# Nine operations moved in a written-out order, and five of 35 warm-up products left out, in a one-core attention and feed-forward kernel

## The chip, the core and the metric

The kernel runs on one core of a Trainium2 chip. The core has a matrix engine (TensorE, PE in the profile; its weight loads are listed apart as PEld), a vector engine (VectorE, DVE), a scalar engine (ScalarE, ACT), GpSimd (POOL) and SyncE (SP), which in this kernel issues nearly all transfers. Each engine works through its own queue in order; engines wait for each other through semaphores. The metric is the device time of one execution in microseconds. The kernel before took 210.79 us (median of three runs, 210.59 to 211.69).

## The reference

Attention over 4 sequences of 768 positions with 8 heads of 64, in which a position sees the 8 first positions and the 95 before it, with a linear bias by distance; then a feed-forward layer, softplus between two products, over the 3072 tokens.

```python
scores = scale * np.matmul(q, k.transpose(0, 1, 3, 2)) + bias      # bias = -slope(head) * distance
scores = np.where(is_global | is_local, scores, -1e9)
a = softmax(scores)                                                # max-subtracted, +1e-9 in the sum
x = np.matmul(a, v)  ->  (3072, 512)                               # heads side by side
h = x @ w_in                                                       # 512 -> 2048
g = np.maximum(h, 0.0) + np.log1p(np.exp(-np.abs(h)))              # softplus
out = g @ w_out                                                    # 2048 -> 512, float32
```

## The kernel before

**Blocks, units, groups.** The tokens are cut into 24 blocks of 128, numbered n = 0 to 23 in the order of work. Two neighbouring blocks of a sequence are a unit (12 units, i); the q, k and v of a unit are loaded together. Block n lies in unit n // 2. Two blocks are also a group (12 groups, g) of the feed-forward layer, whose 256 tokens go through it together. So unit 7 is the blocks 14 and 15, and unit 6 is the blocks 12 and 13, which begin a sequence.

**Names of the operations.** Every piece of work has a name, and the table `ORDER` gives each name an engine (P, V, A, G, S for PE, DVE, ACT, POOL, SP). For a unit i: `ldq`, `ldk`, `ldv` are its loads (L609, 512 KB each, from SP); `castq`, `castk` make bf16 copies (L675, L687); `castv7.11` and its like make the bf16 copy of v in four pieces, the first digit after the dot being the block of the unit and the second one of two halves of its rows (L707); `trq`, `trk7.0`, `trk7.1` are transposing transfers that put q and k into the layout for the products (L837, L830). For a block n: `sc` is its scores product (L950), `z` adds the bias (L976), `ex` the exponential (L983), `pv14.0` and `pv14.1` the products with v for four heads each (L1002, bank `x_ps`), `nm` divides by the sums (L1013, L1014), `xt` transposes the result into `XT` (L1045, a transfer from SP). `gk` and `gv14.0`, `gv14.1` copy the rows of the 8 first positions of the sequence into the k and v of the block before n (L855, L868), so that one pass over that block and n covers the global positions too; `gv14.0` overwrites rows of block 13's v, so it comes after the last reader of them, `pv13.1`.

**The feed-forward layer.** `a5.6` is piece 6 of the first product of group 5 (eight products of 256 columns, L1060, banks `h_ps`); `e` and `ln` are its two activations (L1075, L1086), which leave softplus in bf16 in a tile `g`. The second product runs by Strassen's scheme with seven block products in place of eight: `ka4.1`, `ka4.2`, `ka4.5`, `ka4.6`, `ka4.7` are the five differences of quarters of g that it needs (L452; `ka4.2` and `ka4.5` write one of their own inputs), `b4.1` to `b4.7` are the products (L522, bank `o_ps`), `oe4.1` and its like add them up into the output tile (L483 to L505). The names count groups from 0, so the sums that begin with `ka4` belong to the fifth group of the words in the title of the change.

**What sets the order.** `ORDER` is the whole schedule: the kernel emits the operations in its order, each on the engine that the table names, and nothing reorders them afterwards. An operation waits for the operations whose tiles it reads or overwrites. Moving a word past words of another engine changes nothing but the text; only its place among the words of its own engine counts.

**Warm-up products.** `fill0` to `fill34` (L1234) are products of a tile of zeros, 128 x 512, into bank `x_ps`. Nothing reads them. `fill0` to `fill16` stand at the start, `fill17` to `fill34` between the first blocks of attention.

**Keys of places.** v of unit 7 is loaded by `ldv7`, v of unit 8 by `ldv8`. On POOL the calls from `gv11.0` on are `gv11.0`, two casts of unit 6's v, `castk8.0`, `castv7.11`, `ka4.2`, `ka4.7`, `gv14.0`, `castv8.10`, `castv7.01`, `gv15.0`.

```python
op(f"pv{n}.{part}", "PE", 0.237 if i else 0.12, rank, mm, reads=reads, writes=held([key]), ...)
# reads = [("pb", at), "ones"] + v_keys(n) + (v_keys(prev) if i else [])
op(f"gv{n}.{r}", "POOL", 0.61, rank, fn, reads=[v_keys(first)[r]], writes=[v_keys(prev)[r]], ...)
```

Of the kernel before, what the change touches and what calls it, by code (L numbers as in the profile page):

```python
# [99 lines left out]
a3.2:P ldq6:S trk5.1:S b2.4:P nm8.0:V e3.2:A ka2.1:V ex9.0:A a3.3:P oe2.a:V ln3.0:A pv8.1:P a3.4:P gv9.1:G gk10:V  # L100
ex9.1:A b2.1:P nm8.1:V gv9.0:G ldv6:S ka2.6:V xt8:S e3.3:A pv9.0:P castk6.0:A sc10.0:P ka2.2:G nm9.0:V a3.5:P oe2.1:V
e3.4:A z10.1:V trk6.0:S pv9.1:P e3.5:A b2.5:P ln3.1:A castv5.01:G nm9.1:V a3.7:P castq6.0:G z10.0:V xt9:S ex10.1:A
b2.2:P gk11:G gv10.1:A castv5.10:G a3.6:P ldq7:S oe2.c:V ex10.0:A castv5.00:G trq6:S castv5.11:V sc11.0:P castv6.11:G
e3.6:A gv10.0:V b2.7:P e3.7:A z11.0:V ln3.2:A b2.6:P ldk7:S st1.1.0:S pv10.0:P ex11.0:A a4.0:P nm10.0:V trk6.1:S
z11.1:V a4.1:P e4.0:A pv10.1:P e4.1:A a4.2:P st1.0.0:S gv11.0:G gv11.1:V nm10.1:V ex11.1:A ldv7:S oe2.7:V sc12.0:P
xt10:S castv6.10:G pv11.0:P e4.2:A a4.3:P castv6.00:G nm11.0:V ln3.3:A z12.1:V a4.4:P ln4.0:A castk7.0:V pv11.1:P
z12.0:V b3.3:P e4.3:A ka3.6:V e4.4:A b3.4:P nm11.1:V ex12.0:A ka3.1:V a4.5:P xt11:S ln4.1:A ka3.7:V a4.6:P e4.5:A
castq7.0:V ldq8:S oe3.a:A ka3.5:V sc13.0:P trq7:S ex12.1:A castv6.01:V a4.7:P e4.6:A z13.0:V pv12.0:P b3.1:P e4.7:A
trk7.0:S ln4.2:A a5.0:P oe3.1:V ldk8:S nm12.0:V a5.1:P e5.0:A ldv9:S ka3.2:V ln4.3:A pv12.1:P trk7.1:S b3.5:P gk14:V
ex13.0:A ka4.6:V a5.2:P nm12.1:V e5.1:A b3.2:P ln5.0:A pv13.0:P oe3.c:V a5.3:P st2.1.0:S castk8.0:G e5.2:A nm13.0:V  # L110
st2.0.0:S b3.7:P castv7.00:A z13.1:V ldv8:S castv7.11:G e5.3:A b3.6:P ka4.2:G ex13.1:A sc14.0:P oe3.7:V a5.4:P
castq8.0:A ka4.1:V ka4.7:G b4.3:P ln5.1:A trq8:S z14.1:V a5.5:P gk15:A xt12:S z14.0:V b4.4:P e5.5:A pv13.1:P trk8.0:S
oe4.a:A a5.7:P gv14.0:G nm13.1:V ex14.0:A ka4.5:V castv8.10:G b4.1:P xt13:S e5.4:A sc15.0:P gv14.1:A oe4.1:V
castv7.01:G a5.6:P ex14.1:A st3.0.0:S ldq9:S pv14.0:P e5.6:A ldk9:S b4.5:P nm14.0:V e5.7:A ldv10:S z15.1:V b4.2:P
ln5.2:A pv14.1:P castv9.10:V ln5.3:A a6.0:P gv15.0:G trk8.1:S z15.0:V a6.1:P gk16:G e6.0:A castv7.10:G oe4.c:V
sc16.0:P castq9.0:G e6.1:A a6.2:P ex15.0:A z16.0:V a6.3:P ldk11:S nm14.1:V ex16.0:A st3.1.0:S b4.7:P gv15.1:V gk17:V
z16.1:V e6.3:A b4.6:P castk9.0:A pv15.0:P oe4.7:V a6.5:P e6.2:A ex15.1:A nm15.0:V st4.1.0:S a6.4:P ka5.1:V xt14:S
e6.5:A pv15.1:P b5.3:P e6.4:A gv16.0:G nm15.1:V ln6.0:A gv16.1:V xt15:S b5.4:P castv8.11:V castv8.00:V ln6.1:A
castv8.01:V sc17.0:P ka5.6:V trq9:S a6.6:P oe5.a:A ka5.7:V ln6.2:A castv9.11:V pv16.0:P ka5.5:G trk9.0:S z17.0:V
# [12 lines left out]
gk22:A ex21.0:A a9.4:P oe7.c:V gv21.0:G nm20.1:V gv21.1:A sc22.0:P e9.4:A xt20:S b7.7:P z22.0:V e9.1:A pv21.0:P
ln9.0:A ka8.1:G b7.6:P st6.0.0:S nm21.0:V ex22.0:A a9.3:P oe7.7:V z22.1:V pv21.1:P st7.0.0:S e9.3:A b8.3:P gv22.1:G
# [115 lines left out]
def kernel(  # L249
# [12 lines left out]
    P = nc.NUM_PARTITIONS  # L262
# [969 lines left out]
    def fillers(js):  # L1232
        def fn():
            nc.tensor.matmul(x_ps[:], blank[:, 0:P], blank[:])  # L1234
# [154 lines left out]
```

## Time and profile before

| what | value |
|---|---|
| time, median of three runs (lowest, highest) | 210.79 us (210.59, 211.69) |
| the profiled execution's own time | 211.58 us |
| its span, first to last instruction | 209.8 us |
| PE busy | 201.1 us, 96% |
| ACT busy | 173.1 us, 83% |
| DVE busy | 161.6 us, 77% |
| POOL busy | 100.5 us, 48% |
| granted PE clock | 1.00 |
| idle of PE that a wait ended, longest pieces | 1.2, 1.1, 0.5, 0.5, 0.3, 0.3 us |

The span is measured from the first to the last instruction; 1.8 us of the execution's time lie around it. In rows of a timeline the first column is the start from the beginning of the span, the second the duration, both in us; then come engine, line, operation, the tile written and the tiles read, shapes and a count, and in brackets the engine's idle time just before and what ended it. The end of a product is modelled: the start of the next one tells how long it held the engine.

### The profile page before, as it was taken

To read this page: it belongs to the slowest core of one execution; us is meant where nothing else is said; L and a number is where in the kernel's file an instruction comes from. 1 tells how busy PE (TensorE), PEld (TensorE's weight loads), DVE (VectorE), ACT (ScalarE), POOL (GpSimd) and SP (SyncE) were. 2 spreads that over 40 slices of the span, in tenths; PEclk is the share of its full clock that TensorE was granted. 3 is DMA by queue.
4 is the path that set the end of the run, shared out by engine and by line. 5 is a ranking of instruction groups with operands and counts; after the bars stand their busy time and mean duration, and the time that the engine had idled before them with its cause. 6 is when DMAs were issued, how large, how long until landed. Compare 5 with 4: busy or idle time off the path is not lost.

```text
span 209.8 us, 5505 instructions
## 1 busy us (share of the span) xinstructions
PE 201.1 (96%) x2202; PEld 164.5 (78%) x2211; DVE 161.6 (77%) x306; ACT 173.1 (83%) x251; POOL 100.5 (48%) x106
## 2 busy tenths in 40 slices
PE   7998899999999998999979999999999999999993
PEld 2565786666678887888868888888988989888882
DVE  5878889999789997997869896927897784434373
ACT  4787999899998999989897999779879895897300
POOL 4074682327652683000954169694807506623640
PEclk9999999999999999999999999999999999999999
DMA  5999999999997999999999969985641303200205
GB/s 173 364 362 386 387 358 359 334 227 238 219 209 165 280 188 233 267 203 228 244 158 301 231 113 265 204 155 119 96 82 28 127 3 126 77 0 0 103 21 181
DMA packets 70649, 40.99 MB, mean 195 GB/s; under 512 B 30432, under 2 KB 62688, under 8 KB 70624
## 3 DMA queue, kind: packets, MB, share of 16 engines
q1 hardware_dynamic: 69936, 39.99, 77.7%
q10 hardware_dynamic: 688, 0.66, 1.0%
q8 instruction: 17, 0.28, 0.6%
q14 instruction: 8, 0.07, 0.1%
HBM read 27.26 MB, written 6.29 MB: 160 GB/s over the span
## 4 chain that ended last, share of the span: by engine, by line
PE 67%; DMA 18%; POOL 5%; DVE 3%; SPq 2%; issue 2%; ACTq 0%; POOLq 0%; DVEq 0%
PE h_ps L1060 31%; PE o_ps L522 19%; DMA raw<-in_q_dram 6%; DMA raw<-in_moe_w_in_dram 5%; PE x_ps L1002 4%; PE s_ps L950 4%; PE s_ps L1107 3%; DMA raw<-in_k_dram 3%; PE o_ps L1107 3%; DMA qT<-qb 2%; POOL vb L707 2%; DMA XT<-xs 2%; PE x_ps L522 2%; PE s_ps L522 1%; POOL g L452 1%
## 5 line engine op out<-in xcount | busy, mean ns | idle before, releaser
L1060 PE MATMUL h_ps<-XT,w_in_bf 128*128 128x256 bf16 x768 | 94.6, 273 | 1.2 <-DVE w_in_bf L644 0.5
L1060 PEld LDWEIGHTS <-w_in_bf 128*128 128x128 bf16 x768 | 72.9, 98 | 12.7 <-DVE w_in_bf L644 1.0
L1075 ACT ACTIVATE e<-h_ps 128x512 f32<-128x512 f32 x96 | 59.8, 636 | 14.6 <-PE h_ps L1060 14.0
L1086 ACT ACTIVATE g<-e 128x1024 bf16<-128x1024 f32 x48 | 49.5, 1051 | 0.4
L976 DVE TENSOR_TENSOR z<-s_ps,biasA 128x1024 f32<-128x1024 f32 x38 | 45.7, 1217 | 2.7 <-PE s_ps L950 1.9
L983 ACT ACTIVATE pb<-z 128x1024 bf16<-128x1024 f32 (+1 forms) x44 | 43.5, 993 | 1.7 <-DVE z L976 1.1
L452 POOL TENSOR_TENSOR g<-g 128x1024 bf16<-128x1024 bf16 x12 | 26.0, 2169 | 26.9 <-DVE raw L452 26.6
L522 PEld LDWEIGHTS <-g 128*128 128x128 bf16 x320 | 30.7, 98 | 3.6
L522 PEld LDWEIGHTS <-raw 128*128 128x128 bf16 x240 | 22.9, 98 | 2.8
L522 PE MATMUL o_ps<-raw,raw 128*128 128x256 bf16 x192 | 23.9, 273 | 0.0
L452 DVE TENSOR_TENSOR raw<-g 128x1024 bf16<-128x1024 bf16 x23 | 17.9, 787 | 6.0 <-ACT g L1086 3.9
L452 POOL TENSOR_TENSOR raw<-g 128x1024 bf16<-128x1024 bf16 x7 | 15.3, 2192 | 13.6 <-ACT g L1086 12.2
L1002 PEld LDWEIGHTS <-pb 128*128 128x128 bf16 x352 | 16.4, 97 | 4.7 <-issue 1.3
L522 PE MATMUL o_ps<-raw,g 128*128 128x256 bf16 x160 | 19.8, 273 | 0.0
L868 POOL COPY vb<-vb 4x512 bf16<-4x512 bf16 x20 | 12.6, 630 | 14.5 <-PE x_ps L1002 13.9
L1014 DVE TENSOR_TENSOR xs<-x_ps,rcp 128x256 bf16<-128x256 f32 x40 | 17.0, 424 | 1.4
L1002 PE MATMUL x_ps<-vb,pb 128*128 128x65 bf16 x304 | 15.8, 193 | 1.1 <-POOL vb L707 1.1
L707 POOL CAST vb<-raw 64x512 bf16<-64x512 f32 x22 | 15.1, 686 | 3.0 <-DMA raw<-in_v_dram 1.9
L522 PE MATMUL o_ps<-w_out_bf,g 128*128 128x256 bf16 x128 | 16.1, 273 | 0.0
L1013 DVE RECIPROCAL rcp<-x_ps 128x4 f32<-128x4 f32 x40 | 7.1, 178 | 8.3 <-PE x_ps L1002 7.7
L1234 PE MATMUL x_ps<-blank 128*128 128x512 bf16 x32 | 11.3, 468 | 1.5 <-DVE blank L1159 1.2
L687 POOL CAST kb<-raw 128x1024 bf16<-128x1024 f32 x3 | 3.1, 1035 | 15.6 <-DMA raw<-in_k_dram 15.6
(125 smaller groups left out, 226.5 us busy)
## 6 DMA issues: line engine op xcount, KB each, us to landing
raw<-in_v_dram SPq DMA_DIRECT2D x12, 512.0 KB, 6.2
out_dram<-osb SPq DMA_DIRECT2D x22, 256.0 KB, 3.5
raw<-in_q_dram SPq DMA_DIRECT2D x9, 512.0 KB, 4.8
raw<-in_k_dram SPq DMA_DIRECT2D x9, 512.0 KB, 5.1
raw<-in_moe_w_in_dram SPq DMA_DIRECT2D x8, 512.0 KB, 9.4
raw<-in_moe_w_out_dram SPq DMA_DIRECT2D x8, 512.0 KB, 9.3
raw<-in_k_dram SPq DMA_DIRECT2D x6, 256.0 KB, 5.9
raw<-in_q_dram SPq DMA_DIRECT2D x4, 256.0 KB, 7.2
```

The source lines that it names most:

```text
L452: (nc.vector if eng == "DVE" else nc.gpsimd).tensor_tensor(dst, a[0], b[0], ALU.subtract)
L522: nc.tensor.matmul(psum(j), lhs[:, f // 2, f % 2, :], w(f), start=(f == 0 and not (chain and j in "267")), stop=(f == 7), skip_group_check ...
L707: copy_on[eng](dst, src)
L868: copy_on[eng](vb_of(prev)[sl, :, 0:D], vb_of(first)[sl, :, 0:D])
L976: nc.vector.tensor_tensor(z, src, bias, ALU.add)
L983: nc.scalar.activation(pb[:, 0:nr, :].rearrange("p (y a) b -> p y (a b)", y=2), src, AF.Exp, scale=1.0 / root_d)
L1002: nc.tensor.matmul(xv[:, h, :], pb[:, 4 * (h % 2) + 2 * part + h // 2 if lone else u_all * (2 * (h % 2) + h // 2) + u, :], vb_of(prev if u ...
L1014: nc.vector.tensor_tensor(xs[:, 4 * part : 4 * part + 4, :], xv[:, :, 0:D], rcp[:][:, :, None].to_broadcast([P, 4, D]), ALU.mult,)
L1060: last = nc.tensor.matmul(hv[:, j, :], w_in_bf[:, m, fb * P : fb * P + P], XT[g % NXG][:, m, :], start=(m == 0), stop=(m == NM - 1),)
L1075: nc.scalar.activation(e[:, p % 2, :, :].rearrange("p j (b t r) -> p (j b) r t", b=2, r=2), hb[:].rearrange("p (a r t) -> p a r t", a=4, r=2),
L1086: nc.scalar.activation(gt[:, 2 * p - 2 : 2 * p + 2, :].rearrange("p a t -> p (a t)"), e[:].rearrange("p a j t -> p (a j t)"), AF.Ln, bias=1.0,
L1107: nc.tensor.matmul(bank(key)[:, 0 : z - a], gt[:, fb, ns * P : ns * P + P], w_out_bf[:, fb, a:z], start=(fb == 0), stop=(fb == NFB - 1),)
```

## The change

Five warm-up products are left out of `ORDER`: `fill19`, `fill21`, `fill26`, `fill28`, `fill31`. Nine words stand at other places: `trq6`, `castv6.01`, `castv7.11`, `castv7.01`, `ka4.2`, `ka4.7`, `gv14.0`, `ka4.5` and `oe4.1`. No operation changes its engine, its shape or its inputs. In `fillers` one line is added so that a name that the table leaves out is not made. The words of the table, with those moved or left out:

```diff
@@ warm-up
 fill17:P fill18:P
-fill19:P
 pv0.0:P fill20:P ...
-fill21:P
 trk1.0:P ... fill24:P ... fill25:P ...
-fill26:P
 nm1.0:V ... fill27:P ...
-fill28:P
 gv4.1:G ... fill29:P ... fill30:P ...
-fill31:P
 a0.1:P
@@ transpose of unit 6's q, on SP
 castv5.10:G a3.6:P
+trq6:S
 ldq7:S oe2.c:V ex10.0:A castv5.00:G
-trq6:S
 castv5.11:V sc11.0:P
@@ a cast of unit 6's v, on DVE
 ka3.7:V a4.6:P e4.5:A
+castv6.01:V
 castq7.0:V ldq8:S oe3.a:A ka3.5:V sc13.0:P trq7:S ex12.1:A
-castv6.01:V
 a4.7:P
@@ casts of unit 7's v, sums and copies of the fifth group, on POOL and DVE
 a5.3:P st2.1.0:S
+castv7.11:G castv7.01:G
 castk8.0:G e5.2:A nm13.0:V ... ldv8:S
-castv7.11:G
 e5.3:A b3.6:P
-ka4.2:G
+ka4.7:G
 ex13.1:A sc14.0:P oe3.7:V a5.4:P castq8.0:A ka4.1:V
-ka4.7:G
 b4.3:P ... e5.5:A pv13.1:P
+gv14.0:G ka4.2:G
 trk8.0:S oe4.a:A a5.7:P
-gv14.0:G
 nm13.1:V ex14.0:A
-ka4.5:V
 castv8.10:G b4.1:P
+oe4.1:V ka4.5:V
 xt13:S e5.4:A sc15.0:P gv14.1:A
-oe4.1:V castv7.01:G
 a5.6:P
@@ in fillers
-        for j in js:
+        for j in (x for x in js if f"fill{x}" in PLACED):
```

The changed file is one line shorter, so its line numbers are lower by one than those of the kernel before. In what follows a row names line, operation, the tile written and the tiles read, and the shape.

**POOL, from the last cast of unit 6's v to `castv8.10`.** `vb` is v in bf16; `raw8` holds v of unit 6, `raw0` v of unit 7, `raw7` v of unit 8, `raw2` k of unit 8; the two rows of `TENSOR_TENSOR` are `ka4.2` (in place in g) and `ka4.7` (into `raw12`), the `COPY` is `gv14.0`. The kernel before:

```order
L707 CAST vb_93<-raw8_75 64x8x64 x2
L687 CAST kb0_83<-raw2_69 128x1024
L707 CAST vb_93<-raw0_67 64x8x64
L452 TENSOR_TENSOR g1_108<-g1_108 128x4x2x128
L452 TENSOR_TENSOR raw12_79<-g1_108 128x1024
L868 COPY vb_93<-vb_93 4x8x64
L707 CAST vb_93<-raw7_74 64x8x64
```

The same place now:

```order
L706 CAST vb_93<-raw8_75 64x8x64 x2
L706 CAST vb_93<-raw0_67 64x8x64 x2
L686 CAST kb0_83<-raw2_69 128x1024
L451 TENSOR_TENSOR raw12_79<-g1_108 128x1024
L867 COPY vb_93<-vb_93 4x8x64
L451 TENSOR_TENSOR g1_108<-g1_108 128x4x2x128
L706 CAST vb_93<-raw7_74 64x8x64
```

Two casts of unit 7's v now stand ahead of the cast of unit 8's k; before, one stood behind it and the other (`castv7.01`) behind everything shown. The copy `gv14.0` now has one sum ahead of it where it had two.

**SP, around the transpose of unit 6's q.** `qT0` is the transposed q of unit 6, `raw9` q of unit 7, `raw10` k of unit 7. Before:

```order
L1045 DMA_TRANSPOSE XT4_122<-xs0_101 128x4x128
L609 DMA raw9_76<-in_q_dram 128x8x128
L837 DMA_TRANSPOSE qT0_85<-qb0_81 128x8x128
L609 DMA raw10_77<-in_k_dram 128x8x128
```

Now:

```order
L1044 DMA_TRANSPOSE XT4_122<-xs0_101 128x4x128
L836 DMA_TRANSPOSE qT0_85<-qb0_81 128x8x128
L608 DMA raw9_76<-in_q_dram 128x8x128
L608 DMA raw10_77<-in_k_dram 128x8x128
```

The transpose and the load of unit 7's q have changed places; what stands ahead of the two and behind them is as it was.

More of the change, by code (lines that the diff above doesn't have):

```diff
@@ L100 @@
[L100 to L119, printed above, removed]
@@ new lines @@
+castv5.01:G nm9.1:V a3.7:P castq6.0:G z10.0:V xt9:S ex10.1:A b2.2:P gk11:G gv10.1:A castv5.10:G a3.6:P trq6:S ldq7:S
+oe2.c:V ex10.0:A castv5.00:G castv5.11:V sc11.0:P castv6.11:G e3.6:A gv10.0:V b2.7:P e3.7:A z11.0:V ln3.2:A b2.6:P
+ldk7:S st1.1.0:S pv10.0:P ex11.0:A a4.0:P nm10.0:V trk6.1:S z11.1:V a4.1:P e4.0:A pv10.1:P e4.1:A a4.2:P st1.0.0:S
+gv11.0:G gv11.1:V nm10.1:V ex11.1:A ldv7:S oe2.7:V sc12.0:P xt10:S castv6.10:G pv11.0:P e4.2:A a4.3:P castv6.00:G
+nm11.0:V ln3.3:A z12.1:V a4.4:P ln4.0:A castk7.0:V pv11.1:P z12.0:V b3.3:P e4.3:A ka3.6:V e4.4:A b3.4:P nm11.1:V
@@ new lines @@
+ex12.0:A ka3.1:V a4.5:P xt11:S ln4.1:A ka3.7:V a4.6:P e4.5:A castv6.01:V castq7.0:V ldq8:S oe3.a:A ka3.5:V sc13.0:P
+trq7:S ex12.1:A a4.7:P e4.6:A z13.0:V pv12.0:P b3.1:P e4.7:A trk7.0:S ln4.2:A a5.0:P oe3.1:V ldk8:S nm12.0:V a5.1:P
+e5.0:A ldv9:S ka3.2:V ln4.3:A pv12.1:P trk7.1:S b3.5:P gk14:V ex13.0:A ka4.6:V a5.2:P nm12.1:V e5.1:A b3.2:P ln5.0:A
+pv13.0:P oe3.c:V a5.3:P st2.1.0:S castv7.11:G castv7.01:G castk8.0:G e5.2:A nm13.0:V st2.0.0:S b3.7:P castv7.00:A
+z13.1:V ldv8:S e5.3:A b3.6:P ka4.7:G ex13.1:A sc14.0:P oe3.7:V a5.4:P castq8.0:A ka4.1:V b4.3:P ln5.1:A trq8:S z14.1:V
@@ new lines @@
+a5.5:P gk15:A xt12:S z14.0:V b4.4:P e5.5:A pv13.1:P gv14.0:G ka4.2:G trk8.0:S oe4.a:A a5.7:P nm13.1:V ex14.0:A
+castv8.10:G b4.1:P oe4.1:V ka4.5:V xt13:S e5.4:A sc15.0:P gv14.1:A a5.6:P ex14.1:A st3.0.0:S ldq9:S pv14.0:P e5.6:A
+ldk9:S b4.5:P nm14.0:V e5.7:A ldv10:S z15.1:V b4.2:P ln5.2:A pv14.1:P castv9.10:V ln5.3:A a6.0:P gv15.0:G trk8.1:S
+z15.0:V a6.1:P gk16:G e6.0:A castv7.10:G oe4.c:V sc16.0:P castq9.0:G e6.1:A a6.2:P ex15.0:A z16.0:V a6.3:P ldk11:S
+nm14.1:V ex16.0:A st3.1.0:S b4.7:P gv15.1:V gk17:V z16.1:V e6.3:A b4.6:P castk9.0:A pv15.0:P oe4.7:V a6.5:P e6.2:A
```

102 lines of the change are left out of this document (53 added, 49 removed).

## The prediction

> **What bounds the kernel now.** I read the waits of PE first. PE is busy for 96% of the span at a granted clock of 1.00, so only the pieces in which it stands still, or works on something nobody needs, can be won. Two rows of the view of PE's waits matter here (us in total, times, longest):
>
> ```profile
> PE x_ps L1002 <- POOL vb L707: 1.1, 1, 1.1
> PE h_ps L1060 <- DVE w_in_bf L644: 0.5, 1, 0.5
> ```
>
> The first is one wait for a cast of v on POOL; the second lies in the start-up. The timeline of PE gives their places, and the one wait for a transposed q:
>
> ```profile
> 81.56 1.04 PE L1060 MATMUL h_ps<-XT,w_in_bf 128*128 128x256 bf16 x8
> 83.14 0.40 PE L950 MATMUL s_ps<-qT,kTa 64*128 64x128 bf16 x8 [0.54 <-DMA qT<-qb]
> ...
> 91.77 1.91 PE L1060 MATMUL h_ps<-XT,w_in_bf 128*128 128x256 bf16 x16
> 93.52 0.29 PE L1002 MATMUL x_ps<-vb,pb 128*128 128x65 bf16 x4
> ...
> 103.52 1.03 PE L1060 MATMUL h_ps<-XT,w_in_bf 128*128 128x256 bf16 x8
> 104.40 1.04 PE L522 MATMUL o_ps<-raw,raw 128*128 128x256 bf16 x8
> ...
> 105.92 1.05 PE L1060 MATMUL h_ps<-XT,w_in_bf 128*128 128x256 bf16 x8
> 108.10 0.40 PE L1002 MATMUL x_ps<-vb,pb 128*128 128x65 bf16 x8 [1.14 <-POOL vb L707]
> 108.34 1.91 PE L522 MATMUL o_ps<-w_out_bf,g 128*128 128x256 bf16 x16
> ...
> 110.33 1.91 PE L1060 MATMUL h_ps<-XT,w_in_bf 128*128 128x256 bf16 x16
> ```
>
> Eight products hold PE for 104.40 - 103.52 = 0.88 us. The scores of block 12 (83.14) were due at 81.56 + 0.88 = 82.44, so 0.70 us are lost there; `pv14.0` (108.10) was due at 105.92 + 0.88 = 106.80, so 1.30 us are lost. From 108.10 on no row of PE carries a wait: a microsecond won at 108 should stay won, unless a transfer or another engine then turns out late.
>
> What POOL does before 108 (its timeline):
>
> ```profile
> 82.62 1.28 POOL L707 CAST vb<-raw 64x512 bf16<-64x512 f32 x2
> 99.47 1.03 POOL L687 CAST kb<-raw 128x1024 bf16<-128x1024 f32 x1 [15.58 <-DMA raw<-in_k_dram]
> 100.57 0.96 POOL L707 CAST vb<-raw 64x512 bf16<-64x512 f32 x1
> 101.61 2.13 POOL L452 TENSOR_TENSOR g<-g 128x1024 bf16<-128x1024 bf16 x1
> 103.71 2.12 POOL L452 TENSOR_TENSOR raw<-g 128x1024 bf16<-128x1024 bf16 x1
> 105.78 0.60 POOL L868 COPY vb<-vb 4x512 bf16<-4x512 bf16 x1
> 106.42 1.63 POOL L707 CAST vb<-raw 64x512 bf16<-64x512 f32 x2
> ```
>
> In the order of the table these are two casts of unit 6, `castk8.0`, `castv7.11`, `ka4.2`, `ka4.7`, `gv14.0`, and `castv8.10` with `castv7.01`. POOL idles 15.58 us for k of unit 8 and then runs 8.6 us without a break; the one operation that PE needs, `castv7.01`, is its last, done at 108.05.
>
> **The change, part by part.**
>
> *Five warm-up products.* The group of L1234 on the page, and the chain of waits at the start:
>
> ```profile
> L1234 PE MATMUL x_ps<-blank 128*128 128x512 bf16 x32 | 11.3, 468 | 1.5 <-DVE blank L1159 1.2
> ```
>
> ```profile
> 9.77 10.38 DMA raw<-in_moe_w_in_dram
> ```
>
> At a mean of 0.468 us five of them cost 2.3 us at most. But a load of w_in lands at 9.77 + 10.38 = 20.15, its cast on DVE follows, and PE waits for that (0.5 above). All five stand before that point, on PE alone, so I book 0. The cover is the load: without it up to 2.3 us would be seen. A loss would need a lower clock in the gaps; these are no longer than one product, while PE already idled longer at other places at a clock of 1.00. So 0 on both sides.
>
> *`trq6` ahead of `ldq7`.* SP's timeline:
>
> ```profile
> 77.43 0.52 SPq L609 DMA_DIRECT2D raw<-in_q_dram  x1
> 78.04 1.27 SPq L837 DMA_TRANSPOSE qT<-qb  x1
> ...
> 89.78 1.94 SPq L837 DMA_TRANSPOSE qT<-qb  x1
> ```
>
> The transpose is issued 78.04 - 77.43 = 0.61 us sooner, so the scores of block 12 can come up to 0.61 us sooner. `ldq7` leaves 1.3 us later; its cast is not before 88.97 (below), 10 us on. What stands behind the pair keeps its time. But what follows on DVE hangs on another load, k of unit 7 (first row with its issue, then its landing; the second pair is v of unit 7):
>
> ```profile
> L609 SPq DMA_DIRECT2D raw<-in_k_dram x1: 1099/1099/1099, 79.4 to 79.4; - x1
> DMA to landing us min/median/max: 5.9/5.9/5.9
> ```
>
> ```profile
> L609 SPq DMA_DIRECT2D raw<-in_v_dram x1: 390/390/390, 84.0 to 84.0; - x1
> DMA to landing us min/median/max: 6.0/6.0/6.0
> ```
>
> ```profile
> 85.41 0.69 DVE L687 CAST kb<-raw 128x1024 bf16<-128x1024 f32 x1 [0.24 <-issue]
> ...
> 88.97 0.69 DVE L675 CAST qb<-raw 128x1024 bf16<-128x1024 f32 x1
> 89.57 0.68 DVE L452 TENSOR_TENSOR g<-g 128x1024 bf16<-128x1024 bf16 x1
> 90.28 0.42 DVE L707 CAST vb<-raw 64x512 bf16<-64x512 f32 x1
> ...
> 92.84 0.42 DVE L1014 TENSOR_TENSOR xs<-x_ps,rcp 128x256 bf16<-128x256 f32 x1
> ...
> 99.93 1.12 DVE L452 TENSOR_TENSOR raw<-g 128x1024 bf16<-128x1024 bf16 x1
> 100.98 2.34 DVE L976 TENSOR_TENSOR z<-s_ps,biasA 128x1024 f32<-128x1024 f32 x2
> ...
> 106.85 0.67 DVE L486 TENSOR_TENSOR osb<-osb,o_ps 128x512 f32<-128x512 f32 x1
> ```
>
> k7 lands at 79.4 + 5.9 = 85.3, DVE casts it at 85.41, and then runs practically without a pause to 92.84 + 0.42 = 93.26, where `nm12.0` frees bank `x_ps` for `pv12.1` (93.52 on PE). The same work in any order ends no sooner. So of the 0.61 us only 93.52 - 93.26 = 0.26 get past this place.
>
> *`castv6.01` two places up on DVE.* `pv12.0` needs it; it ended at 90.70, just when PE came to it. Now it ends near 89.4 and lets PE be early. The price is its 0.42 us on `castq7.0` and `ka3.5` behind it, and so on `trq7` (89.78), on the transposes and the load of unit 8's k behind that on SP: POOL's `castk8.0` slips from 99.47 towards 99.9. PE does not wait for any of these by itself.
>
> *Two casts of unit 7's v into POOL's idle time.* v7 lands at 84.0 + 6.0 = 90.0, so both (0.64 us each, from 1.28 for two) run from about 90.0 to 91.3, when POOL had nothing to do. They are not free: VectorE and POOL slow each other. `ka4.1` (99.93) took 1.12 beside `castk8.0`, where `ka3.5` alone took 0.68, so 0.44 more; it ended 0.55 after the cast had (101.05 against 100.50). The z sums (2.34 for two) beside POOL's sum are not slowed against any other. In the new order DVE does `castq7.0` to about 90.1, then `ka3.5`, then z: so it is `ka3.5` that can be hit, inside the unbroken run that ends at `nm12.0`. From below 0 (`ka3.5` goes first), from above 1.28 (v7 lands 0.7 us sooner, and each cast stops one DVE operation). I take 0.3, between 0 and the 0.44 of the row. With the 0.26 won there, PE reaches `pv12.1` 0.04 later than before: nothing, with ends of -0.26 and +1.02.
>
> [...]
>
> *`ka4.7` before `gv14.0`, `ka4.2` after it; `oe4.1` before `ka4.5`.* POOL after `castk8.0` (now to about 100.9): `ka4.7` to 103.1; `gv14.0` waits for `pv13.1`, which PE has issued before 103.52, and is done near 104.3; `ka4.2` to 106.5. `pv14.0` needs no more of POOL after 104.3. The other half of that copy is ACT's:
>
> ```profile
> 105.57 0.62 ACT L868 COPY vb<-vb 4x512 bf16<-4x512 bf16 x1
> ```
>
> done at 106.19. So `pv14.0` can start at 106.80: 1.30 us won. `ka4.2` was done at 103.74 and is now done at 106.5; its product `b4.2` is due at 106.80 + 0.24 + 0.88 = 107.92. `ka4.5` needs `ka4.7`, 2.7 us earlier now. It comes behind `oe4.1`, which waits for `b4.1` (104.40 + 0.88 = 105.28) and takes 0.67: `ka4.5` ends between 106.7 and 107.1 (0.68 to 1.12). `b4.5` is due at 107.04. I book 0.1.
>
> **Sum:** 0 + 0 - 1.3 + 0.1 = -1.2 us: span 209.8 to 208.6, the profiled execution 211.58 to 210.4. That execution is 0.79 above the median of the runs shown, inside their spread; the same step from 210.79 gives **209.6 us**, 0.6% less. About 0.5%, 1.05 us, is what a measurement of this kernel can tell from no change.
>
> **The rivals.**
>
> *The port takes it (chance 0.22).* Each of the two casts stops DVE once in the run to `nm12.0`. For: the 0.44 above, and that v7's landing (90.0) is within 0.1 of `castq7.0`'s end. Against: z and `nm` are not touched. PE comes to `pv12.1` later by 0.4 (one cast, 0.64 - 0.26) to 1.0, and -1.2 becomes -0.9 to -0.2: 209.9 to 210.6, say 210.3.
>
> *Slower: the transposed output of block 13 comes late (0.08).* `a6.0` (110.33) reads what `xt13` brings (the second row is its landing, the third the spread of nine such transfers from 59 to 125 us):
>
> ```profile
> L1045 SPq DMA_TRANSPOSE XT<-xs x1: 1822/1822/1822, 105.3 to 105.3; - x1
> DMA to landing us min/median/max: 3.3/3.3/3.3
> ...
> DMA to landing us min/median/max: 2.6/3.6/6.1
> ```
>
> It lands at 108.6, and `a6.0` is now due at 110.33 - 1.2 = 109.1: 0.5 us of room where there were 1.7. It decides once the transfer takes over 3.8 us. At 6.1 us it lands at 111.4, and PE is 1.1 us later than before: 211.9. Against: the loads around it leave no earlier before 106 us.
>
> *The room is used up elsewhere (0.08).* `xt13` at 4.9 us, or `ka4.5` stopped by POOL's `ka4.2` for its whole 2.1: the gain goes, 210.8.
>
> **How the numbers follow.** The forecast has the remaining 0.62; its own range is 209.2 (0.26 more from `pv12.1`, no port cost) to 210.0. Four fifths of it lie beyond 0.5%, and a tenth of the first rival: faster 0.52. Within 0.5%: a fifth of the forecast, the rest of the first rival, the third: 0.40. Slower 0.08. The range reaches into the first and third rival: 209.0 to 210.9.
>
> **What would show it.** Right: the wait of PE for POOL's L707 is gone; the waits for qT and, still, for w_in; POOL casts v near 90 and 91; PE reaches `pv12.1` within 0.3 us of 93.52 and `pv14.0` near 106.8. Wrong: DVE's `ka` near 90 longer than 1.2 us, a new wait of PE before XT or behind DVE between 93 and 110, or a PE that reaches 20.9 at another time than before.

## The result, and the profile after

| kernel | median (lowest to highest), us | executions |
|---|---|---|
| before, same chip, same rounds | 211.14 (210.49 to 211.98) | 7 |
| after | 209.78 (209.08 to 210.76) | 7 |

The ratio is 0.9941 with a 95% interval of 0.9914 to 0.9967: 0.59% less, 1.24 us of 211.14. The forecast was 209.6 and -1.2 us. The profiled execution took 209.4 us with a span of 207.6, where the kernel before had 211.58 and 209.8.

The view of PE's waits, kernel after (us in total, times, longest):

```profile
PE h_ps L1059 <- DVE w_in_bf L643: 0.3, 1, 0.3
PE h_ps L1059 <- POOL w_in_bf L643: 0.3, 1, 0.3
...
PE h_ps L1059 <- DMA XT<-xs: 0.2, 1, 0.2
```

The wait for POOL's cast of v (1.1) is gone, and so is the one for qT. The wait for w_in on DVE is there still. PE's timeline, kernel after, at the places that the prediction names:

```profile
20.60 1.05 PE L1059 MATMUL h_ps<-XT,w_in_bf 128*128 128x256 bf16 x8 [0.30 <-DVE w_in_bf L643]
...
81.14 1.04 PE L1059 MATMUL h_ps<-XT,w_in_bf 128*128 128x256 bf16 x8
82.11 0.40 PE L949 MATMUL s_ps<-qT,kTa 64*128 64x128 bf16 x8
...
92.45 0.29 PE L1001 MATMUL x_ps<-vb,pb 128*128 128x65 bf16 x4
...
104.85 1.05 PE L1059 MATMUL h_ps<-XT,w_in_bf 128*128 128x256 bf16 x8
105.73 0.41 PE L1001 MATMUL x_ps<-vb,pb 128*128 128x65 bf16 x8
105.98 1.91 PE L521 MATMUL o_ps<-w_out_bf,g 128*128 128x256 bf16 x16
...
107.96 1.25 PE L1059 MATMUL h_ps<-XT,w_in_bf 128*128 128x256 bf16 x10
```

No row from 81 to 108 carries a wait. `pv14.0` (105.73) follows the start of the eight products ahead of it by 0.88 us; before it followed by 2.18. The starts of the same piece of work in both traces, and what each stretch gained:

| piece on PE | before | after | difference | gained since the row above |
|---|---|---|---|---|
| third piece of the first product of group 0, behind the cast of w_in | 20.92 | 20.60 | -0.32 | 0.32 |
| scores of block 12 | 83.14 | 82.11 | -1.03 | 0.71 |
| `pv12.1` | 93.52 | 92.45 | -1.07 | 0.04 |
| `pv14.0` | 108.10 | 105.73 | -2.37 | 1.30 |
| end of the span | 209.8 | 207.6 | -2.2 | -0.17 |

One profile stands against one here, and the same transfer takes another time in each: the load of w_in ahead of the first row took 10.38 us in the one and 9.76 in the other. Two rows of the kernel before, from its PE timeline, are such differences:

```profile
20.92 1.05 PE L1060 MATMUL h_ps<-XT,w_in_bf 128*128 128x256 bf16 x8 [0.51 <-DVE w_in_bf L644]
...
64.19 1.03 PE L1060 MATMUL h_ps<-XT,w_in_bf 128*128 128x256 bf16 x8 [0.33 <-DMA XT<-xs]
```

The first piece starts at 20.43 to 20.92 in the seven profiles here of kernels with all warm-up products, and at 20.60 to 21.15 in the six without the five: the 0.32 is chance. At 64.19 the kernel before waits for a transposed output; the kernel after has no wait at that piece, though nothing was changed there, and has one of 0.2 for another transposed output at 79. So the 2.2 us between the two spans hold differences that are not the change's, and the 1.24 from the timings is the measure of it. On POOL, kernel after (timeline):

```profile
82.20 1.27 POOL L706 CAST vb<-raw 64x512 bf16<-64x512 f32 x2
89.33 1.75 POOL L706 CAST vb<-raw 64x512 bf16<-64x512 f32 x2 [5.87 <-DMA raw<-in_v_dram]
98.31 1.04 POOL L686 CAST kb<-raw 128x1024 bf16<-128x1024 f32 x1 [7.23 <-DMA raw<-in_k_dram]
99.32 2.57 POOL L451 TENSOR_TENSOR raw<-g 128x1024 bf16<-128x1024 bf16 x1
102.65 0.60 POOL L867 COPY vb<-vb 4x512 bf16<-4x512 bf16 x1 [0.77 <-PE x_ps L1001]
103.23 2.12 POOL L451 TENSOR_TENSOR g<-g 128x1024 bf16<-128x1024 bf16 x1
105.42 0.96 POOL L706 CAST vb<-raw 64x512 bf16<-64x512 f32 x1
```

The two casts of unit 7's v run at 89.33, as soon as v lands, inside what was one idle stretch of 15.58 us. `gv14.0` ends at 103.25, 2.48 us before `pv14.0`; POOL is no longer what PE waits for.

### The profile page after: what moved, and what is told of

Its sections match the earlier page's. It is cut to its first block, busy times and chain, and to the rows that moved or that the text cites. A ratio compares the mean times of both kernels' runs of the same rounds, so it can differ in the third digit from the quotient of the medians.

```text
span 207.6 us, 5495 instructions
## 1 busy us (share of the span) xinstructions
PE 200.7 (97%) x2197; PEld 164.3 (79%) x2206; DVE 161.7 (78%) x306; ACT 172.8 (83%) x251; POOL 101.4 (49%) x106
## 4 chain that ended last, share of the span: by engine, by line
PE 83%; DMA 10%; DVE 3%; SPq 1%; issue 1%; POOL 1%; ACTq 0%; DVEq 0%; POOLq 0%
PE h_ps L1059 40%; PE o_ps L521 24%; DMA raw<-in_moe_w_in_dram 5%; PE s_ps L949 5%; PE x_ps L1001 5%; PE o_ps L1106 3%; PE s_ps L1106 3%; DMA raw<-in_q_dram 3%; DMA XT<-xs 2%; PE x_ps L521 2%; PE s_ps L521 1%; SPq L639 1%; DVE z L975 1%; POOL w_in_bf L643 1%; DVE osb L504 0%
## 5 line engine op out<-in xcount | busy, mean ns | idle before, releaser
L451 POOL TENSOR_TENSOR g<-g 128x1024 bf16<-128x1024 bf16 x12 | 26.0, 2171 | 26.4 <-DVE raw L451 26.2
L521 PEld LDWEIGHTS <-g 128*128 128x128 bf16 x320 | 30.6, 98 | 3.6
L521 PEld LDWEIGHTS <-raw 128*128 128x128 bf16 x240 | 22.9, 98 | 2.9
L521 PE MATMUL o_ps<-raw,raw 128*128 128x256 bf16 x192 | 23.9, 273 | 0.0
L451 DVE TENSOR_TENSOR raw<-g 128x1024 bf16<-128x1024 bf16 x23 | 18.9, 833 | 6.0 <-ACT g L1085 3.9
L451 POOL TENSOR_TENSOR raw<-g 128x1024 bf16<-128x1024 bf16 x7 | 15.8, 2256 | 13.6 <-ACT g L1085 12.1
L521 PE MATMUL o_ps<-raw,g 128*128 128x256 bf16 x160 | 19.8, 273 | 0.0
L521 PE MATMUL o_ps<-w_out_bf,g 128*128 128x256 bf16 x128 | 16.1, 273 | 0.0
L1233 PE MATMUL x_ps<-blank 128*128 128x512 bf16 x27 | 10.7, 501 | 1.4 <-DVE blank L1158 1.2
L674 POOL CAST qb<-raw 128x1024 bf16<-128x1024 f32 x6 | 6.6, 1100 | 7.3 <-DMA raw<-in_q_dram 5.7
```

The lines of the kernel that those rows point to most:

```text
L451: (nc.vector if eng == "DVE" else nc.gpsimd).tensor_tensor(dst, a[0], b[0], ALU.subtract)
L521: nc.tensor.matmul(psum(j), lhs[:, f // 2, f % 2, :], w(f), start=(f == 0 and not (chain and j in "267")), stop=(f == 7), skip_group_check ...
```

## The experiments

Each ratio is against the kernel before on the same chip, run in the same rounds; each edit is told against the kernel before or against the change. The two casts are `castv7.11` and `castv7.01`.

### One part at a time

**Only the five warm-up products left out** (products of zeros; nothing else is changed in the kernel before).

```diff
 fill17:P fill18:P
-fill19:P
... the same for fill21, fill26, fill28 and fill31
```

> Only the five warm-up products are left out; the nine operations stand where they stood. Theory (the start-up is bound by the load of w_in that lands near 20.15): PE reaches the product after that load (20.92 before) at 20.9 give or take the landing itself, time within 0.2 us of the kernel before. Rival (the products were on the path, since in the changed kernel PE was 0.32 us ahead at 20.6): 0.3 to 0.5 us faster, and PE ahead by that at 60 us too. Second rival (the clock or the fills' gaps cost something): slower, with products of 128 x 256 taking longer than 0.11 us between 12 and 20.

Measured: 210.74 us against 210.49, ratio 1.0015 (0.9992 to 1.0037). Its PE waits and its PE timeline:

```profile
PE h_ps L1059 <- DVE w_in_bf L643: 0.9, 1, 0.9
PE o_ps L521 <- POOL g L451: 0.7, 1, 0.7
PE s_ps L949 <- DMA qT<-qb: 0.4, 1, 0.4
```

```profile
20.62 1.05 PE L1059 MATMUL h_ps<-XT,w_in_bf 128*128 128x256 bf16 x8 [0.93 <-DVE w_in_bf L643]
```

What PE saves it waits out at 20.62, behind the load of w_in: 0.93 us there instead of 0.51. The products are worth nothing. The other two rows come back below.

**Only `trq6` and `castv6.01` moved.**

```diff
+trq6:S
 ldq7:S oe2.c:V ex10.0:A castv5.00:G
-trq6:S
...
+castv6.01:V
 castq7.0:V ldq8:S oe3.a:A ka3.5:V sc13.0:P trq7:S ex12.1:A
-castv6.01:V
```

> Only trq6 and castv6.01 are moved. Theory as the prediction had it (VectorE's run from the landing of unit 7's k to nm12.0 lets 0.26 of 0.61 us past): the 0.70 us lost before the scores of block 12 gone, 0.3 us gained at pv12.1, and nothing at 108: pv14.0 waits for castv7.01 as before, 0.25 us sooner at most; time 0 to 0.3 us less. Rival (all 0.61 us get past, as in the profile of the changed kernel): pv12.1 0.6 us sooner, but the wait at 108 for POOL then grows by 0.6 us, since castv7.01 hangs on the landing of unit 8's k: 0 gained in the end. Either way the wait of PE for POOL's cast is 1.1 us or more.

Measured: 210.60 us against 210.49, ratio 1.0011 (0.9990 to 1.0031). The wait for qT is gone and PE reaches `pv12.1` at 92.28, 1.24 us sooner than in the kernel before; then (POOL's timeline, and PE's):

```profile
98.46 1.04 POOL L686 CAST kb<-raw 128x1024 bf16<-128x1024 f32 x1 [15.15 <-DMA raw<-in_k_dram]
...
105.40 1.63 POOL L706 CAST vb<-raw 64x512 bf16<-64x512 f32 x2
```

```profile
107.08 0.40 PE L1001 MATMUL x_ps<-vb,pb 128*128 128x65 bf16 x8 [1.35 <-POOL vb L706]
```

The wait for POOL is longer than before (1.35 against 1.14). POOL's chain starts when k of unit 8 has landed, and takes as long as it did; a PE that comes sooner waits longer. Here the stall removed in front of another one that hangs on a load gave nothing by itself.

**Only the POOL and DVE words moved**: `castv7.11`, `castv7.01`, `ka4.2`, `ka4.7`, `gv14.0`, `ka4.5`, `oe4.1`, as in the change.

> Only the casts castv7.11 and castv7.01, the sums ka4.2, ka4.7, ka4.5, the copy gv14.0 and oe4.1 are moved. Theory: the 1.30 us at pv14.0 are gone, the 0.70 us before the scores of block 12 stay: 1.2 to 1.4 us less than before, which is nearly all that the whole change gave (1.24 to 1.36). Rival (the parts need each other): 0.9 us or less.

Measured: 209.51 us against 210.49, ratio 0.9957 (0.9933 to 0.9981). No wait at `pv14.0`, which starts at 105.64. The ratio is 0.9 us less, with an interval of 0.4 to 1.4, so the time does not tell the theory (1.2 to 1.4) from the rival (0.9 or less). `trq6` was not moved, yet its qT came in time in this profile.

**Only the two casts moved.**

```diff
+castv7.11:G castv7.01:G
 castk8.0:G e5.2:A nm13.0:V ... ldv8:S
-castv7.11:G
...
 xt13:S e5.4:A sc15.0:P gv14.1:A oe4.1:V
-castv7.01:G
```

> Only the two casts of unit 7's v are moved ahead of castk8.0; ka4.2, ka4.7, gv14.0, ka4.5 and oe4.1 stay. Theory (the casts alone made PE wait): after castk8.0 at 100.5 the two sums end near 104.8 and gv14.0 near 105.4, before pv14.0 is due at 106.8, so 1.2 to 1.4 us less, as with the whole POOL part. Rival (the sums had to change places too, since gv14.0 behind both of them comes after 106.8, or ka4.5, which waits for ka4.7, holds b4.5): 0.3 to 0.9 us less, with PE waiting before pv14.0 for gv14.0 or before b4.5 for ka4.5.

Measured: 209.93 us against 210.49, ratio 0.9975 (0.9946 to 1.0003): 0.5 us less where 1.2 to 1.4 were expected, and by its time alone not clear of no gain. On PE's timeline the wait at `pv14.0` is gone with these two words alone, the sums and the copy being where they were:

```profile
105.11 1.05 PE L1059 MATMUL h_ps<-XT,w_in_bf 128*128 128x256 bf16 x8
105.99 0.41 PE L1001 MATMUL x_ps<-vb,pb 128*128 128x65 bf16 x8
```

Neither of the rival's waits, before `pv14.0` or before `b4.5`, is in this profile. Why the time gained less than the theory said is not shown.

**The two casts and `trq6`**: three words of the change in the kernel before.

> Of the whole change only castv7.11, castv7.01 and trq6 are moved. Theory (these three carry the gain; the sums ka4.2, ka4.7, ka4.5, the copy gv14.0, oe4.1, castv6.01 and the warm-up products carry none of it): a ratio of 0.994 to 0.997 as for the whole change, no wait of PE for the transposed q at 83 nor for POOL at 108. Rival (the rest is needed): 0.998 or more, with a wait of PE before pv12.0, before pv14.0 for gv14.0, or before b4.5.

Measured: 209.52 us against 210.88, ratio 0.9948 (0.9924 to 0.9973). No wait at 83 nor at 108. The ratio of the whole change lies in this interval, and this ratio in that of the whole change: three of the nine words carry what can be measured, and the five products and the other six words add nothing that these runs can tell.

### Is it the landing of k8?

**The kernel before with `ldk8` moved up, and nothing else.** POOL keeps its old order, `castv7.01` last.

```diff
 sc13.0:P
+ldk8:S
 trq7:S ... trk7.0:S ln4.2:A a5.0:P oe3.1:V
-ldk8:S
 nm12.0:V
```

> The kernel before with one word moved: the load of unit 8's k stands two places earlier on SP, ahead of the transposes of unit 7's q and k; no cast is moved. Theory (PE waited at 108 because POOL's 8.6 us of work begin when that load lands): the load lands near 95 in place of 99.3, castv7.01 ends before 106.5 though it is still POOL's last, the wait of PE at pv14.0 is under 0.3 us, and the ratio is 0.995 to 0.998. Rival (POOL is then held by something else, v of unit 8 for castv8.10 or gv14.0's wait for pv13.1): the wait stays above 0.8 us and the time is that of the kernel before.

Measured: 209.67 us against 210.88, ratio 0.9961 (0.9938 to 0.9985). POOL's timeline, and PE's:

```profile
94.72 1.03 POOL L686 CAST kb<-raw 128x1024 bf16<-128x1024 f32 x1 [11.26 <-ACT pb L982]
...
102.97 0.60 POOL L867 COPY vb<-vb 4x512 bf16<-4x512 bf16 x1 [2.22 <-PE x_ps L1001]
103.61 1.64 POOL L706 CAST vb<-raw 64x512 bf16<-64x512 f32 x2
```

```profile
106.10 0.41 PE L1001 MATMUL x_ps<-vb,pb 128*128 128x65 bf16 x8
```

One load, issued at 88.73 instead of 93.14, does the same as the whole change, as far as these runs can tell. Nothing on POOL was put ahead of anything; its work merely starts at 94.72 instead of 99.47. (The row names ACT as what ended the idle time; the longest of the three landings of loads from 86 to 94 is 5.8 us, so the load landed by 88.73 + 5.8 = 94.5, just ahead of the start.) `castv7.01`, still POOL's last, ends at 105.25, 0.85 us before `pv14.0`. This is the sharpest evidence for the mechanism: `castv7.01` was late because POOL's chain waited for k8, not because POOL had too much to do.

**The kernel before once more**, one profile.

> The kernel before once more, for a second profile. Theory (the wait at pv14.0 is what the landing of unit 8's k leaves of it and differs from run to run): a wait there between 0.1 and 1.4 us, equal to that landing + 8.7 us less the time at which PE comes to pv14.0. Rival (a fixed wait): 1.1 to 1.2 us again.

Measured: 211.23 us, one execution. POOL's timeline and PE's:

```profile
98.27 1.03 POOL L687 CAST kb<-raw 128x1024 bf16<-128x1024 f32 x1 [14.55 <-DMA raw<-in_k_dram]
...
105.22 1.63 POOL L707 CAST vb<-raw 64x512 bf16<-64x512 f32 x2
```

```profile
106.90 0.40 PE L1002 MATMUL x_ps<-vb,pb 128*128 128x65 bf16 x8 [0.76 <-POOL vb L707]
```

The chain from the start of `castk8.0` to the end of `castv7.01` takes 8.58 us here (98.27 to 106.85) and took 8.58 in the first profile (99.47 to 108.05). It moves as a block with the landing, and whether PE waits depends on when PE arrives. Over the four profiles with the old POOL order and the old load the wait of PE was 1.14, 0.12, 1.35 and 0.76 us, in the order before, without the five products, with `trq6` and `castv6.01` moved, before again: 0.84 on average. The profile that the prediction read had drawn one of the larger values.

The same holds for qT. In the six profiles with `trq6` at its old place PE waited 0.54, 0.44, 0, 0.18, 0.26 and 0 us for it, 0.24 on average; in the eight with it moved, never. The two averages add up to 1.08 us, near the 1.24 of the timing; they come from few profiles. That `trq6` is needed beside the casts is not proved by this: the kernel with the POOL and DVE words alone came out as fast as the whole.

### What the other words do

**The change once more**, for its time and a second profile.

> The changed kernel itself, beside the others of this call. Theory: the whole change gives what its POOL part alone gave, a ratio of 0.993 to 0.997 to the kernel before. Rival (the parts add to each other): 0.991 to 0.994, since the other parts alone were at 1.001 and gave nothing.

Measured: 209.54 us against 210.77, ratio 0.9959 (0.9937 to 0.9980). In this profile v of unit 7 lands half a us sooner, at 88.8, and the casts on POOL meet `ka3.5` on DVE (DVE's timeline):

```profile
88.41 0.69 DVE L674 CAST qb<-raw 128x1024 bf16<-128x1024 f32 x1
89.01 1.10 DVE L451 TENSOR_TENSOR g<-g 128x1024 bf16<-128x1024 bf16 x1
```

`ka3.5` takes 1.10 instead of 0.68. PE is not held by it at `pv12.1` (92.53, no wait): it comes there 10.35 us after the scores of block 12 (82.18), as in the first profile of the change (92.45 - 82.11 = 10.34).

**The change, and v of unit 7 loaded earlier**, so that both casts on POOL meet DVE for certain.

```diff
 ldk7:S st1.1.0:S ... nm10.0:V
+ldv7:S
 trk6.1:S z11.1:V ... ex11.1:A
-ldv7:S
 oe2.7:V
```

> The changed kernel with the load of unit 7's v two places earlier on SP (ahead of trk6.1), so that the two casts of POOL fall wholly into VectorE's run between the landing of unit 7's k and nm12.0, near 87.5 to 88.8. It moves trk6.1 and a store back by 0.5 us. The port rival as the prediction priced it: VectorE's casts and sums in that stretch take 0.3 to 0.6 us longer each where a cast of POOL runs, nm12.0 comes 0.6 to 1.2 us later after castk7.0 than the 7.07 us of the changed kernel, and PE waits at pv12.1: 0.3 to 1.0 us slower than the changed kernel. Theory after the profiles (the operation that VectorE has in hand goes on and POOL's cast is stopped, so VectorE loses at most 0.3 per cast): 7.1 to 7.7 us, under 0.3 us slower.

Measured: 209.81 us against 210.77, ratio 0.9959 (0.9941 to 0.9976). The casts run on POOL from 87.81; DVE's timeline:

```profile
88.46 0.73 DVE L706 CAST vb<-raw 64x512 bf16<-64x512 f32 x1
89.22 0.99 DVE L674 CAST qb<-raw 128x1024 bf16<-128x1024 f32 x1
```

Beside each cast one operation on DVE takes longer: `castv6.01` takes 0.73 instead of 0.42 and `castq7.0` 0.99 instead of 0.69, 0.61 us together. The first operation of `nm12.0` starts 92.46 - 84.79 = 7.67 us after `castk7.0`, inside the theory's 7.1 to 7.7. PE pays a little of it: from the scores of block 12 (82.60) to `pv12.1` (93.15) it takes 10.55 us, 0.21 more than in the change. That is less than the rival's 0.3 to 1.0, and the ratio is that of the change. So POOL's casts do cost DVE time, and PE pays a third of it here.

**The change with `castv6.01` back at its old place.**

```diff
-castv6.01:V
 castq7.0:V ldq8:S oe3.a:A ka3.5:V
+castv6.01:V
 sc13.0:P trq7:S
```

> The changed kernel with castv6.01 back behind ka3.5. Theory (pv12.0 then waits for it, since it ended 0.06 us before PE came to it, and PE is now earlier against VectorE): a wait of PE of 0.2 to 0.6 us before pv12.0 near 90, time 0 to 0.4 us more than the changed kernel. Rival (PE is not that early, as in the run with the POOL part alone, which had no such wait): no wait, same time within 0.2 us.

Measured: 210.02 us against 210.77, ratio 0.9981 (0.9956 to 1.0006). In its profile PE has no wait at `pv12.0` (89.50), and the span of 207.2 is the shortest of all the profiles. The interval overlaps those of the change, so whether the move of `castv6.01` is worth some tenths stays open; the profile shows no place where it would be.

**The change with `ka6.5` moved from POOL to DVE.** In several of the profiles above a sum of group 6 on POOL, `ka6.5`, holds PE near 139 (the row `PE o_ps L521 <- POOL g L451` of the first experiment, 0.7 us). If it took back part of the gain, moving it would show.

```diff
-ka6.5:G
 trk10.0:S ...
+ka6.5:V
 oe6.1:V
```

> The changed kernel with one more move: the sum ka6.5 goes from POOL (2.13 us, behind two casts that wait for the load of unit 11's v) to VectorE, just ahead of oe6.1, where VectorE idles 1.2 to 2.4 us. Theory (what was won at 108 is given back in part at b6.5, near 138, in runs in which that load lands late: PE waited there 0.14 to 0.74 us in three of four profiles of single parts, and had no room in the changed kernel): no wait of PE at b6.5, 0.2 to 0.6 us less than the changed kernel. Rival (b6.5 costs nothing once the whole change is in, or the next transfer takes its place): the same as the changed kernel within 0.2 us.

Measured: 209.58 us against 210.77, ratio 0.9963 (0.9940 to 0.9986). No wait there, but the change alone had none either, in both of its profiles. Nothing is gained.

**The change without any of the remaining warm-up products from `fill17` on** (13 more products of zeros are not computed).

```diff
-fill17:P fill18:P
 pv0.0:P
-fill20:P
... the same for fill22 to fill25, fill27, fill29, fill30 and fill32 to fill34
```

> The changed kernel without any of the 18 warm-up products between the first blocks of attention (fill17 to fill34); the first 17 stay. Theory (all of them lie before the landing of w_in near 20 and cost nothing, and gaps of under a microsecond do not lower the clock): the same time as the changed kernel within 0.2 us, PE's wait for w_in longer by up to 2 us, the granted clock at 1.00, and products of 128 x 65 and 128 x 128 between 12 and 20 as long as before. Rival (the clock falls in the gaps): products after 20 of twice the length for some us, 1 to 4 us slower.

Measured: 210.24 us against 210.88, ratio 0.9984 (0.9958 to 1.0010). Here the clock falls. The first two rows are from the windows of this kernel (stretch, its length, PE's busy time, granted clock, DMA's share, GB/s), the next two from its PE timeline:

```profile
18.57:21.98 3.41, 1.61 (x21) 1.00 1.05 387
21.98:25.39 3.41, 3.41 (x31) 0.50 1.05 386
```

```profile
20.49 1.05 PE L1058 MATMUL h_ps<-XT,w_in_bf 128*128 128x256 bf16 x8 [1.79 <-DVE w_in_bf L642]
...
23.33 1.91 PE L1058 MATMUL h_ps<-XT,w_in_bf 128*128 128x256 bf16 x8
25.03 0.57 PE L1000 MATMUL o_ps<-vb,pb 128*128 128x65 bf16 x8
```

Eight products that take 0.88 us elsewhere take 25.03 - 23.33 = 1.70. At the scores that follow, PE is 1.28 us later than in the kernel after (25.54 against 24.26); at 41 us it is 1.12 later (41.14 against 40.02). So the first five products cost nothing to leave out, and without the other thirteen the clock can fall; what that is worth stands in the last section.

## Why the prediction was right, step by step

**The wait at `pv14.0`: right, in mechanism and place.** 1.30 us were booked and 1.30 came (108.10 - 93.52 = 14.58 before, 105.73 - 92.45 = 13.28 after). That the wait hangs on POOL's chain behind k8 is shown by the kernels with the casts ahead of it and with k8 alone: in each of them the wait is gone. What the step left out is that this 1.30 was one drawing. The wait is k8's landing plus 8.6 us less the time at which PE arrives; counted as the prediction counts it, against the time at which `pv14.0` was due, it was 1.30, 0.30, 1.52 and 0.92 us in the four profiles with the old order of POOL and the old load.

**`trq6`: the step came as booked, the limit behind it did not.** From the piece ahead of them to the scores of block 12 PE takes 82.11 - 81.14 = 0.97 us where it took 1.58. That is the 0.61 that was named as the most; the other 0.42 of the 1.03 in the table was won ahead of this place, by differences that are not the change's. But "only 93.52 - 93.26 = 0.26 get past this place" failed: from these scores to `pv12.1` PE takes 10.34 us where it took 10.38, so all of the 0.61 got past. The limit rested on k of unit 7 landing at 85.3. SP's timeline of the kernel after, and the landing of the two loads (the longest is that of k of unit 7):

```profile
76.67 1.26 SPq L836 DMA_TRANSPOSE qT<-qb  x1
78.03 0.53 SPq L608 DMA_DIRECT2D raw<-in_q_dram  x1
78.65 0.57 SPq L608 DMA_DIRECT2D raw<-in_k_dram  x1
```

```profile
DMA to landing us min/median/max: 4.8/5.3/5.8
```

k of unit 7 leaves at 78.65 instead of 79.40 and lands at 78.65 + 5.8 = 84.45 instead of 85.3. The move did not do this. From the start of the pair on SP to the issue of k it takes 78.65 - 76.67 = 1.98 us where it took 79.40 - 77.43 = 1.97, so "What stands behind the pair keeps its time" held; the pair as a whole began 0.76 us sooner. In the kernel before, run once more with nothing moved, it began sooner still (SP's timeline):

```profile
76.07 0.52 SPq L609 DMA_DIRECT2D raw<-in_q_dram  x1
...
78.17 0.85 SPq L609 DMA_DIRECT2D raw<-in_k_dram  x1
```

In the thirteen other profiles the pair begins between 76.03 and 77.06; the 77.43 that the prediction read is the latest of all. With k7 earlier, the unbroken run on DVE begins sooner (DVE's timeline, kernel after):

```profile
84.52 0.69 DVE L686 CAST kb<-raw 128x1024 bf16<-128x1024 f32 x1 [0.39 <-issue]
...
88.19 0.42 DVE L706 CAST vb<-raw 64x512 bf16<-64x512 f32 x1
88.65 0.69 DVE L674 CAST qb<-raw 128x1024 bf16<-128x1024 f32 x1
89.26 0.69 DVE L451 TENSOR_TENSOR g<-g 128x1024 bf16<-128x1024 bf16 x1
...
91.80 0.42 DVE L1013 TENSOR_TENSOR xs<-x_ps,rcp 128x256 bf16<-128x256 f32 x1
...
105.06 0.84 DVE L451 TENSOR_TENSOR g<-g 128x1024 bf16<-128x1024 bf16 x1
```

`nm12.0` ends at 92.22, 1.04 us sooner. Its run takes 7.70 us from the start of `castk7.0` where it took 93.26 - 85.41 = 7.85, so 0.15 us of the run read as unbroken were pauses. In thirteen of the fourteen profiles PE takes 10.34 to 10.38 us from the scores of block 12 to `pv12.1`, with `trq6` moved or not. So the limit bound in none of these; whether it would with k7 as late as 85.3 and PE 0.61 us sooner, no run shows. What the move is worth varies as the wait at 108 does: in the six profiles with `trq6` at its old place the scores of block 12 come 0.70, 0.60, 0.42, 0.33, 0.09 and 0.09 us after they were due, against 0.09 with it moved, 0.28 us on average.

**Two of the signs failed, and one of being wrong came.** PE was to reach `pv12.1` within 0.3 us of 93.52 and `pv14.0` near 106.8; it reached them at 92.45 and 105.73. It came past the load of w_in at 20.60, which the prediction had put down as a sign of being wrong if it was not 20.9. The 1.07 us at `pv12.1` are the 0.42 from ahead of 81, the 0.61 of `trq6` and 0.04 from there on.

**The port: the size right for DVE, wrong for PE.** 0.3 us was booked, between 0 and 1.28. In the nine profiles with the two casts in their new place DVE lost 0 once (the first of the change: 0.69 for `ka3.5` above), 0.31 to 0.42 seven times, and 0.61 where v was loaded earlier. The prediction passed the 0.3 on to PE; but PE comes to `pv12.1` 10.34 to 10.36 us after the scores of block 12 in eight of the nine, as without the casts, and 0.21 later only where v was loaded earlier. So the rival "The port takes it", priced at 0.4 to 1.0 us of PE, did not come even there. (Its near end, 0.4, makes of -1.2 a -0.8 and 210.0, not the -0.9 and 209.9 that it gives.) No run shows a port, or what else makes the two engines slow each other; what the runs show is that both take longer side by side. On DVE these are two casts and a sum: 0.73 us where `castv6.01` takes 0.42 alone, 0.99 where `castq7.0` takes 0.69, 1.10 where `ka3.5` takes 0.68. On POOL the two casts take 1.75 us at 89.33 where two took 1.27 at 82.20. DVE lost 0.30 to 0.42 us an operation, less than the full 0.64 of a cast; what sets that size no run here tests.

**The five warm-up products: right**, 0 within what their run can tell (1.0015, 0.9992 to 1.0037), with the load of w_in as the cover. "A loss would need a lower clock in the gaps" was the right condition, and "no longer than one product" was not reason enough to dismiss it: with all 18 out the clock does fall in some executions, to 0.50 in the one profiled, after a wait of 1.79 us.

**`castv6.01`, the sums and the copy: nothing measurable.** They were booked at 0 or inside other steps. `ka4.5` starts at 105.06 (above) and ends at 105.90, 0.08 us before its product at 105.98; the 0.1 booked for it did not come. The slip of `castk8.0` to 99.9 did not come either: with SP's queue ahead of before, it starts at 98.31.

**The rival on XT.** "0.5 us of room" for `a6.0` proved about 0.46: the transfer was issued at 103.90, took 3.6 us to its landing at 107.5, and `a6.0` started at 107.96 without a wait. It stayed harmless, and its condition, over 3.8 us, was not met.

**The sum.** -1.2 was booked and -1.24 measured; the mechanism of its main term is shown, but that the two numbers are so near is partly luck. Three profiles have both `trq6` and POOL's order as before: the kernel before twice, and the one without the five products. In them `pv14.0` came 1.30, 0.92 and 0.30 us after it was due, 0.84 on average, not 1.30. The scores of block 12 came 0.61, 0 and 0.51 us later than with `trq6` moved, 0.37 on average, where the prediction had nothing (0.26 less 0.3 for the port). Together that is 1.21 us. One term booked too large and one too small cancel; and 0.1 booked for `ka4.5` did not come.

## What to carry to other kernels

When a stall ends at an operation that is last in an engine's queue, find what the head of that queue waits for; if that is a load, either let independent work pass ahead of it or issue the load sooner; here both gave the same, 0.9957 with the casts and the words around them moved and 0.9961 with the load, as far as the runs can tell. Size a stall that hangs on a load from several profiles, because one profile gives one drawing of the landing. The same holds for a limit: the one put on `trq6` stood on a single late issue of a load, and the other profiles did not have it. And look for the next load-bound stall before booking the gain of the first.

## What the runs showed of the hardware

**The clock fell after a wait of 1.79 us, in some executions.** Without the 18 products PE was busy for 1.61 of the 3.41 us from 18.57 to 21.98, nearly all the rest being one wait of 1.79, and the granted clock was 0.50 for the next 3.41 us. The kernel after and the one without five products only, over the same stretch (windows, one kernel each):

```profile
18.57:21.98 3.41, 3.04 (x29) 1.00 1.06 390
```

```profile
18.57:21.98 3.41, 2.42 (x24) 1.00 1.05 387
```

At 3.04 and 2.42 busy it stayed at 1.00, with a wait of 0.93 inside the second. Whether the length of one wait or the busy share of a stretch decides, these runs do not separate. The stretch was cut to end where the clock fell. By windows of one us the clock was 0.98 from 21 to 22, 0.50 from 22 to 25 and 0.81 from 25 to 26; if it was 0.50 or 1.00 at every moment, it was down for 3.4 us, an estimate. It does not fall each time: the mean clock over an execution was 0.991 or 0.992 in three of the twelve executions without the 18 products (210.94 to 211.62 us; 1.7 us lost of 209 is 0.8%) and 0.997 or more in the other nine (median 209.95, mean 210.18), as in the other kernels here (0.996 to 1.000). The mean of the three is 211.25, so the price of the fall is about 1.1 us, an estimate, in a quarter of these executions. What decides in which executions it falls, no run here tests.

**The same load takes another time in each execution.** k of unit 8 took 6.33, 5.63, 5.85 and 6.23 us from its issue to the start of its cast on POOL in the four profiles with the old POOL order (in the first of them 6.19 to the landing), and was issued between 92.04 and 93.14. The stall of PE that hangs on it varied by 1.2 us, though POOL's chain from the start of `castk8.0` to the end of `castv7.01` took 8.55 to 8.58 us in all four.
